# A channel-attention and ELU feed-forward kernel: joins of W' in two acts, the first pair's three v blocks cast on ScalarE, two output transfers in later units

## The chip, the cores and the metric

The kernel runs on 1 core of a Trainium2 chip. The core has five engines with a queue of instructions each: TensorE (PE; PEld is its weight load), VectorE (DVE), ScalarE (ACT), GpSimd (POOL) and SyncE (SP). SP and POOL issue nearly all the transfers here; one that casts or adds goes through POOL. An instruction waits at the head of its engine's queue, and everything behind it waits too. The metric is device time in microseconds (us). Before the change three runs took 2078.13, 2079.51 and 2080.13 us, median 2079.51.

## The reference

```python
qn = q / (np.linalg.norm(q, axis=1, keepdims=True) + 1e-06)      # q, k, v: (4, 6080, 256)
kn = k / (np.linalg.norm(k, axis=1, keepdims=True) + 1e-06)
s = kn.transpose(0, 2, 1) @ qn / tau                             # 256 x 256 for each batch
a = softmax(s)
x = (v @ a).reshape(24320, 256)
h = x @ w_in                                                     # w_in: (256, 2048)
g = np.where(h > 0, h, np.exp(np.minimum(h, 0)) - 1)
out = g @ w_out                                                  # w_out: (2048, 256)
```

The inputs q, k and v are float32. The kernel multiplies a and w_in first: W' = a w_in (256 x 2048 for each batch), so that h = v W'.

## The kernel before

Every float32 operand of a large product is split into a high part (rounded to the matrix format, fp32r) and a low part (the rest), and a product is three matmuls: high x high, high x low and low x high. High parts come from a ScalarE cast or from a casting transfer of GpSimd; low parts are a VectorE subtraction that reads the high part. Tokens go in 52 chunks of up to 512, 13 to a batch; W' has 16 blocks of 128 columns, in four quarters fq of 512.

Three stages matter here.

- **The opening** (to about 65 us) computes the attention matrix of batch 0 and the first quarter of W'.
- **64 steps** (`take`, 0 to 63) run the first four chunks the plain way. A step multiplies one block of W' with a chunk of v (`h_item`, L446 to L448: six matmuls into `ph`), applies ELU (ScalarE L457 and L458, VectorE L459), splits the block before it (`split_g`: ScalarE L114, VectorE L115) and multiplies the block three steps back with w_out (`out_item`, L486 to L490). What else has to be done, such as converting weights, squaring and adding batch 1's rows or preparing the next stage, is given to steps by `at(step, fn)`. Within a step the order of the code is the order of the queues.
- **Units**: the remaining 48 chunks go in 24 pairs of chunks (blocks of v B11, B12, B21, B22, and sums of them T1 to T4) against sums of W' blocks (S1 to S4, and A11, A12, A22), with seven products instead of eight. A pair has eight units (fq, j); a unit computes four blocks of h with `product` (L1161), applies ELU (L1238, L1239, L1242), splits the result (casting transfer L1256, low parts L1263 one unit later) and multiplies the unit before with w_out (L1171 to L1173). Between these, a planner puts side tasks into slots: `task(engine, cost, fn, deps, when, level, late, due)`; `when` is the earliest time (a unit has 4), lower levels go first, and a dependency may carry a gap. Each `spend(engine, budget, now)` in a unit issues what is ready.

The change touches what leads from the steps to the units:

- `join(fq)`: W' of batch 0 lies as high and low part in `wp`; the sums need it whole, so `x` (tiles x_0 to x_3 by fq) gets the high part by a copy of SyncE (L919, 512 KB) and the low part by an adding transfer of GpSimd (L920, 512 KB), which waits for the copy to land. Joins 0 and 1 stand in step 47, join 2 in step 59, join 3 is a planner's task. `s_sum` (VectorE, L844 to L847) then forms S1 to S4 in x, `s_hi` (GpSimd, L853, two casting transfers) and `s_lo` (VectorE, four subtractions L859) split the seven matrices into s_0 to s_3.
- The first pair: `first_pair_loaded` (step 45) loads v into two `exact` tiles, `hi_of` makes the high parts (of B22, B11 and B21 by a casting transfer out of HBM, L1086, in steps 47 to 49; of the T sums by ScalarE, L1088), `lo_of` (L1094) the low parts in steps 50 to 52, `t_sum` (L1074 to L1077) the T sums.
- `copy_out` for the last chunk of the steps adds two halves of 256 KB to the output with a transfer of GpSimd (L1191), issued where the copy out of PSUM is made, in unit 1.
- Also on GpSimd's queue: `add_row` (L875), which adds squares of batch 1 in this stage, and later the same by the planner (L1432).

The pools hand out room in rotation. s_0 takes the tile that held the first two quarters of W', s_2 that of the other two, s_3 that of `scr`, out of which the outputs of the first chunks go.

Of the kernel before, what the change touches and what calls it, by code (L numbers as in the profile page):

```python
# [7 lines left out]
F32 = mybir.dt.float32  # L8
# [3 lines left out]
ALU = mybir.AluOpType  # L12
# [42 lines left out]
def channel_attention_then_elu_ffn(ctx: ExitStack, tc, q, k, vT, tau, w_in, w_out, outT):  # L55
# [8 lines left out]
    nc = tc.nc  # L64
# [655 lines left out]
    def at(step, fn, free=False):  # L720
        (loose if free else side).setdefault(step, []).append(fn)
# [98 lines left out]
    def new_x(b, fq):  # L820
        if b > 0 and fq % 2 == 1:
            halves_of_x = [work.tile([P, 4, HF], F32, tag="raw", bufs=5, name=f"x_{b}_{fq}_{y}") for y in range(2)]
        else:
            x = work.tile([P, 8, HF], F32, tag="qk", bufs=3, name=f"x_{b}_{fq}")
            halves_of_x = [x[:, 0:4], x[:, 4:8]]
        state[b, "x", fq] = halves_of_x
# [58 lines left out]
    for x, g in enumerate((*range(KEPT, EARLY), *range(KEPT))):  # L885
        y = 10 + SPACING * x
# [25 lines left out]
    at(39, load_first_w)  # L912
    at(42, split_first_w)

    def join(fq):
        new_x(0, fq)
        wp = wps[0][fq]
        to = state[0, "x", fq][0].rearrange("p (k h) n -> p k (h n)", k=KT)
        nc.sync.dma_start(to, wp[:, :, 0].bitcast(F32))  # L919
        nc.gpsimd.dma_start(to, wp[:, :, 1].bitcast(F32), accum_op=ALU.add)  # L920

    at(47, lambda: join(0))
    at(47, lambda: join(1))
    for y in range(4):
        at(51 + y // 2, lambda y=y: s_sum(0, 0, y))
        at(56 + y // 2, lambda y=y: s_sum(0, 1, y))
    at(53, lambda: (new_s(0), room.append(spares[0]), [s_hi(0, 0, *p, True) for p in ((0, 3), (3, SPARE))]))
    for y, p in enumerate(PARTS):
        at(59 + y, lambda p=p: s_lo(0, 0, *p))
    at(59, lambda: join(2))  # L930

    steps = [(c, f) for c, lo, hi in pieces for f in range(lo, hi)]
    es, gs, pos = {}, {}, {}
# [51 lines left out]
    def task(engine, cost, fn, deps=(), when=0, level=1, late=None, due=None):  # L985

        t = Task(fn, tuple(d for d in deps if d is not None), when)
        t.late, t.engine = late, engine
        t.cost, t.due = cost, due
        if due is not None:  # L990
            level = 0
        queues[engine, level].append(t)
        return t
# [78 lines left out]
    def t_sum(p, k):  # L1072
        (
            lambda: nc.vector.tensor_sub(of(p, "T3"), of(p, "B22"), of(p, "B12")),  # L1074
            lambda: nc.vector.tensor_sub(of(p, "T1"), of(p, "B12"), of(p, "B11")),
            lambda: nc.vector.tensor_add(of(p, "T2"), of(p, "T3"), of(p, "B11")),
            lambda: nc.vector.tensor_sub(of(p, "T4"), of(p, "B21"), of(p, "T2")),  # L1077
        )[k]()

    def hi_of(p, term):  # L1080
        t0, n = columns(p)
        operands[p, term] = [room.pop(0)]
        to = operands[p, term][0][:, 0:n]
        if term in BLOCKS:
            kt, x = BLOCKS[term]
            nc.gpsimd.dma_start(to, vT[kt * P : kt * P + P, t0 + x * n : t0 + x * n + n])  # L1086
        else:
            nc.scalar.copy(to, of(p, term))  # L1088

    def lo_of(p, term):  # L1090
        n = columns(p)[1]
        operands[p, term].append(room.pop(0))
        hi, lo = (x[:, 0:n] for x in operands[p, term])
        nc.vector.tensor_sub(lo, of(p, term), hi.bitcast(F32))  # L1094
# [14 lines left out]
        room.extend(cut_up(work.tile([P, 4 * CH], F32R, tag="vt", bufs=2, name="t_0"), 4))  # L1109

    at(45, first_pair_loaded)
    at(47, first_pair_room)
    at(50, first_pair_next)
    for y, term in enumerate(("B22", "B11", "B21")):
        at(47 + y, lambda term=term: hi_of(0, term))
        at(50 + y, lambda term=term: lo_of(0, term))
    for y in range(4):
        at((53, 53, 55, 55)[y], lambda y=y: t_sum(0, y))
    at(57, first_pair_more)
    for x, y, term in ((56, 57, "T3"), (57, 59, "T2"), (58, 60, "T1"), (60, None, "T4")):  # L1120
        at(x, lambda term=term: hi_of(0, term))
# [64 lines left out]
    def copy_out(c, dt):  # L1186
        _, t0, n = span(c)
        if c < M:
            o, to = half[c][:, dt, 0:n], outT[dt * P : dt * P + P, t0 : t0 + n]
            nc.scalar.copy(quarters(o), quarters_of_turns(out_bank(c, dt)[:, 0:n]))  # L1190
            nc.gpsimd.dma_start(to, o, accum_op=ALU.add)  # L1191
            return
        assert all(len(y) == 2 for y in operands.values())
        x = exacts[dt][:, (c - M) % 2 * CH : (c - M) % 2 * CH + CH]
        o, to = x[:, 0:n], outT[dt * P : dt * P + P, t0 : t0 + n]
        if c == NCH - 1 and dt == DT - 1:
            m = n // 2
            y, z = o.rearrange("p (r t) -> p r t", r=2), out_bank(c, dt)[:, 0:n].rearrange("p (q r s) -> p r s q", r=2, s=2)
            y = y.rearrange("p r (s q) -> p r s q", s=2)
            nc.vector.tensor_copy(y[:, 0], z[:, 0])  # L1200
            nc.scalar.copy(y[:, 1], z[:, 1])
            nc.sync.dma_start(to[:, 0:m], o[:, 0:m])
            nc.scalar.dma_start(to[:, m:n], o[:, m:n])
        else:
            nc.scalar.copy(quarters(o), quarters_of_turns(out_bank(c, dt)[:, 0:n]))
            nc.sync.dma_start(to, o)
# [99 lines left out]
    def plan_s(b, fq, t, norm_deps, early=False):  # L1306
# [21 lines left out]
        hi = {}  # L1328
        if early and fq > 1:
            if fq == 3:  # L1330
                x = task(SP, 0, lambda: join(3), [(prior["lo before"], 1)], when=t, level=0, late=0)
            for k in range(4):
                x = task(DVE, 0.415, lambda k=k: s_sum(b, fq, k), [x and (x, 5) if k == 0 else x], when=t, due=t + 4, late=1)

# [405 lines left out]
```

## Time and profile before

| | before |
|---|---|
| median of 3 runs | 2079.51 us |
| the profiled execution | 2079.67 us, span 2077.9 us |
| DVE, ACT, POOL busy | 77%, 69%, 30% of the span |
| mean granted TensorE clock | 0.998 |
| transfers of POOL (q0) | 154592 packets, 295.05 MB |
| s<-x, 16 transfers of 512 KB, issue to landing | 4.9 us (median) |
| x<-wp of POOL, 4 transfers of 512 KB | 5.9 us (median) |

The span goes from the first to the last instruction. Busy time counts an engine while it executes; the idle time before an instruction is put down to what released it last. A row of the timeline gives start, duration, engine, line, operation, the tile written and the tiles read, and in brackets the idle time before it and its releaser. `x<-wp` means that x is written and wp read.

The 25 us stretches around the end of the steps (step 63 ends at 252 us, units follow) show TensorE's busy time with its matmuls, then PEld, DVE, ACT and POOL, the granted clock, the DMA engines' busy share and GB/s:

```profile
200.00:225.00 25.00, 18.86 (x86) 15.91 (x85) 15.11 (x23) 14.44 (x26) 7.33 (x9) 0.93 0.97 253
225.00:250.00 25.00, 25.00 (x109) 21.60 (x109) 24.23 (x43) 17.88 (x32) 1.42 (x2) 0.93 0.35 109
250.00:275.00 25.00, 23.41 (x105) 19.23 (x105) 19.95 (x35) 17.59 (x31) 9.75 (x15) 1.00 0.82 246
275.00:300.00 25.00, 20.58 (x88) 17.38 (x87) 17.56 (x31) 12.21 (x20) 8.60 (x17) 0.93 0.75 218
300.00:325.00 25.00, 25.00 (x118) 21.89 (x117) 22.73 (x37) 16.60 (x28) 5.70 (x11) 1.00 0.48 151
```

From 300 us on nearly every such stretch has TensorE busy throughout.

### The profile page before, as it was taken

The page shows a single profiled execution, that of the slowest core. Times are in us where ns is not written, and L with a number is a line of the kernel's source. Part 1 is how long each engine was busy: PE and PEld are TensorE (multiplying, and loading weights), DVE is VectorE, ACT ScalarE, POOL GpSimd, SP SyncE. Part 2 cuts the span into 40 slices and gives each one's busy share as a digit, 9 for nine tenths or more (in the row PEclk, how much of TensorE's full clock was granted, in tenths as well). Part 3 has the DMA queues.
Part 4 walks back from the last instruction along what each step waited for, and adds up shares of the span by engine and source line. Part 5 has one row for each costly group of instructions (what it writes and reads, how often), then busy time and mean ns, then how long its engine had stood idle before and what let it go on. Part 6 is the DMA issues. An engine that isn't in the chain of part 4 may idle for free.

```text
span 2077.9 us, 30137 instructions
## 1 busy us (share of the span) xinstructions
PE 2060.1 (99%) x9961; PEld 1826.6 (88%) x9961; DVE 1592.1 (77%) x2520; ACT 1429.2 (69%) x2420; POOL 625.5 (30%) x1084
## 2 busy tenths in 40 slices
PE   9999889999999999999999999999999999999999
PEld 8888778898888888888998888888998888888998
DVE  7878777777878777777778777777778867767775
ACT  6878657677666676766766667676776666666675
POOL 0011133442222444443222344443322222222221
PEclk9999999999999999999999999999999999999999
DMA  9357685994676989987457598997645653553533
GB/s 368 125 153 206 179 233 178 265 249 133 187 221 183 273 222 285 254 235 210 143 185 231 164 286 240 253 278 203 195 158 191 196 160 109 168 161 107 171 119 118
DMA packets 213339, 415.47 MB, mean 200 GB/s; under 512 B 23232, under 2 KB 68928, under 8 KB 211136
## 3 DMA queue, kind: packets, MB, share of 16 engines
q0 software_dynamic: 154592, 295.05, 50.2%
q1 hardware_dynamic: 58448, 118.39, 17.5%
q8 instruction: 78, 1.28, 0.3%
q14 instruction: 77, 0.63, 0.1%
q10 hardware_dynamic: 144, 0.13, 0.0%
HBM read 145.29 MB, written 30.15 MB: 84 GB/s over the span
## 4 chain that ended last, share of the span: by engine, by line
PE 92%; DMA 4%; issue 3%; DVE 1%; ACT 1%; POOL 0%; POOLq 0%; SPq 0%; DVEq 0%
PE bank_b L1161 16%; PE po L1172 14%; PE po L1173 14%; PE po L1171 14%; PE bank_e L1161 11%; PE bank_a L1161 11%; PE gram L225 4%; PE gram L574 2%; DMA sum<-raw 2%; PE pe L574 1%; PE ph L446 1%; PE ph L448 1%; PE ph L447 1%; PE po L490 1%; PE pw L816 0%
## 5 line engine op out<-in xcount | busy, mean ns | idle before, releaser
L1173 PE MATMUL po<-g,wo 128*128 128x512 f32 (+1 forms) x1416 | 535.3, 378 | 0.0
L1172 PE MATMUL po<-t,wo 128*128 128x512 f32 (+1 forms) x968 | 366.0, 378 | 0.0
L1171 PE MATMUL po<-t,wo 128*128 128x512 f32 (+1 forms) x968 | 365.0, 377 | 0.0
L1634 DVE TENSOR_TENSOR bank_e<-bank_b,p 128x512 f32<-128x512 f32 (+1 forms) x176 | 122.0, 693 | 282.0 <-PE bank_b L1161 271.5
L1173 PEld LDWEIGHTS po<-g,wo 128*128 128x128 f32 x1416 | 267.9, 189 | 34.6
L1624 ACT COPY bank_b<-bank_a 128x512 f32<-128x512 f32 (+1 forms) x176 | 99.5, 565 | 272.0 <-PE bank_a L1161 265.4
L1239 ACT ACTIVATE other<-other 128x512 f32<-128x512 f32 (+1 forms) x396 | 248.0, 626 | 12.6
L1256 POOL DMA_DIRECT2D t<-other x242 | 130.2, 538 | 419.3 <-DVE other L1242 256.3
L1256 POOL DMA_DIRECT2D t<-held x242 | 130.6, 542 | 287.8 <-DVE held L1242 117.6
L1171 PEld LDWEIGHTS po<-t,wo 128*128 128x128 f32 x968 | 183.0, 189 | 23.6
L1172 PEld LDWEIGHTS po<-t,wo 128*128 128x128 f32 x968 | 183.1, 189 | 22.6
L1239 ACT ACTIVATE held<-held 128x512 f32<-128x512 f32 (+1 forms) x308 | 193.2, 627 | 9.8
L1161 PE MATMUL bank_b<-t,s 128*128 128x512 f32 (+1 forms) x576 | 194.5, 379 | 5.1 <-DVE p L1651 5.1
L225 PE MATMUL gram<-qk 128*128 128x256 f32 x708 | 193.0, 273 | 0.0
L1256 POOL DMA_DIRECT2D g<-other x154 | 82.9, 539 | 326.9 <-DVE other L1242 182.1
L1172 PE MATMUL po<-g,wo 128*128 128x512 f32 (+1 forms) x448 | 170.4, 380 | 0.0
L1171 PE MATMUL po<-g,wo 128*128 128x512 f32 (+1 forms) x448 | 169.7, 379 | 0.0
L1263 DVE TENSOR_TENSOR g<-held,t 128x512 fp32r<-128x512 f32 (+1 forms) x242 | 162.2, 678 | 5.9 <-DMA t<-held 5.6
L1263 DVE TENSOR_TENSOR g<-other,t 128x512 fp32r<-128x512 f32 (+1 forms) x242 | 162.6, 679 | 0.5 <-DMA t<-other 0.5
L1238 ACT ACTIVATE other<-bank_a 128x512 f32<-128x512 f32 (+1 forms) x132 | 78.1, 592 | 117.1 <-PE bank_a L1161 112.5
L1161 PE MATMUL bank_b<-g,s 128*128 128x512 f32 (+1 forms) x432 | 147.1, 377 | 0.5 <-ACT bank_b L1624 0.5
L225 PEld LDWEIGHTS gram<-qk 128*128 128x128 f32 x708 | 135.4, 191 | 4.5
(288 smaller groups left out, 4920.7 us busy)
## 6 DMA issues: line engine op xcount, KB each, us to landing
t<-held POOLq DMA_DIRECT2D x154, 256.0 KB, 3.0
t<-other POOLq DMA_DIRECT2D x154, 256.0 KB, 2.7
acc<-raw POOLq DMA_DIRECT2D x118, 256.0 KB, 5.3
g<-other POOLq DMA_DIRECT2D x98, 256.0 KB, 2.3
t<-held POOLq DMA_DIRECT2D x88, 248.0 KB, 2.2
t<-other POOLq DMA_DIRECT2D x88, 248.0 KB, 2.2
raw<-in_q_dram SPq DMA_DIRECT2D x76, 256.0 KB, 3.6
raw<-in_k_dram SPq DMA_DIRECT2D x76, 256.0 KB, 4.2
```

Of the source, the lines that this page charges most:

```text
L225: yield nc.tensor.matmul(gram[:, ct, :], hl[:, x, 1, r, cs], in_turns(hl[:, y, 0, r, :]), start=(first and ct == 0 and r == 0 and k == 0), ...
L574: nc.tensor.matmul(gram[ct], raw[:, 1, r, ct * P : ct * P + P], raw[:, 0, r, :], start=first[ct], stop=last[ct])
L1161: nc.tensor.matmul(bank[:, 0:n], w[:, x], y, start=(begin and k == 0), stop=(k == 2), skip_group_check=True)
L1171: yield nc.tensor.matmul(o, wo[:, f, 0, ds], hi, start=begin, stop=False)
L1172: yield nc.tensor.matmul(o, wo[:, f, 1, ds], hi, start=False, stop=False)
L1173: yield nc.tensor.matmul(o, wo[:, f, 0, ds], lo, start=False, stop=end)
L1238: nc.scalar.activation(e, h, AF.Relu, scale=-1.0)
L1239: nc.scalar.activation(e, e, AF.Exp, scale=-1.0)
L1256: nc.gpsimd.dma_start(hi, e)
L1263: nc.vector.tensor_sub(lo, e, hi.bitcast(F32))
L1624: nc.scalar.copy(vb, va)
L1634: nc.vector.tensor_add(ve, vb, vp)
```

## The change

Three edits. (1) A join becomes two acts: the copy, and two steps later the adding transfer; copies now in steps 45, 47 and 59, additions in 47, 49 and 61; join 3's addition is a planner's task of GpSimd at level 0 that follows the copy by a gap of 2. (2) ScalarE casts the high parts of B22, B11 and B21 in steps 50 to 52 instead of three casting transfers in steps 47 to 49; their low parts come one step later (51 to 53), the t sums in steps 54, 55, 55 and 56, and the room for them is taken in step 50. (3) The two output transfers become tasks with earliest times 10 and 14, in units 2 and 3.

```diff
-    def join(fq):
-        new_x(0, fq)
+    def join(fq, x):
+        if x == 0:
+            new_x(0, fq)
         wp = wps[0][fq]
         to = state[0, "x", fq][0].rearrange("p (k h) n -> p k (h n)", k=KT)
-        nc.sync.dma_start(to, wp[:, :, 0].bitcast(F32))
-        nc.gpsimd.dma_start(to, wp[:, :, 1].bitcast(F32), accum_op=ALU.add)
-
-    at(47, lambda: join(0))
-    at(47, lambda: join(1))
+        if x == 0:
+            nc.sync.dma_start(to, wp[:, :, 0].bitcast(F32))
+        else:
+            nc.gpsimd.dma_start(to, wp[:, :, 1].bitcast(F32), accum_op=ALU.add)
+
+    for fq, y in enumerate((45, 47, 59)):
+        at(y, lambda fq=fq: join(fq, 0))
+        at(y + 2, lambda fq=fq: join(fq, 1))
...
-    at(59, lambda: join(2))
...
-    def hi_of(p, term):
+    def hi_of(p, term, by_act=False):
...
-        if term in BLOCKS:
+        if term in BLOCKS and not by_act:
...
-    at(47, first_pair_room)
+    at(50, first_pair_room)
     at(50, first_pair_next)
     for y, term in enumerate(("B22", "B11", "B21")):
-        at(47 + y, lambda term=term: hi_of(0, term))
-        at(50 + y, lambda term=term: lo_of(0, term))
+        at(50 + y, lambda term=term: hi_of(0, term, True))
+        at(51 + y, lambda term=term: lo_of(0, term))
     for y in range(4):
-        at((53, 53, 55, 55)[y], lambda y=y: t_sum(0, y))
+        at((54, 55, 55, 56)[y], lambda y=y: t_sum(0, y))
...
-            nc.gpsimd.dma_start(to, o, accum_op=ALU.add)
+            task(POOL, 0.6, lambda: nc.gpsimd.dma_start(to, o, accum_op=ALU.add), when=(10, 14)[dt], level=0)
...
-                x = task(SP, 0, lambda: join(3), [(prior["lo before"], 1)], when=t, level=0, late=0)
+                x = task(SP, 0, lambda: join(3, 0), [(prior["lo before"], 1)], when=t, level=0, late=0)
+                x = task(POOL, 0.6, lambda: join(3, 1), [(x, 2)], when=t, level=0)
```

Code behind the edits has moved by three or four lines (L1256 is L1259 after, L1094 is L1097). How the queues stand, at three places:

GpSimd's queue from step 47 on; x_0 and x_1 are the joins' tiles, acc<-raw the adding of squares, t<-in_v_dram the casts of the first pair, s the first split matrices. Before:

```order
L920 DMA x_0_1700<-wp_380 128x2x512
L920 DMA x_1_1703<-wp_380 128x2x512
L875 DMA acc_1728<-raw_712 128x512
L1086 DMA t_1706<-in_v_dram 128x512 x2
L875 DMA acc_1728<-raw_712 128x512
L1086 DMA t_1706<-in_v_dram 128x512
L853 DMA s_1848<-x_0_1700 128x768
```

and now:

```order
L923 DMA x_0_1639<-wp_380 128x2x512
L923 DMA x_1_1703<-wp_380 128x2x512
L875 DMA acc_1725<-raw_712 128x512 x2
L853 DMA s_1847<-x_0_1639 128x768
L875 DMA acc_1725<-raw_711 128x512 x2
```

The three casts have left this queue; the two adding transfers still stand one behind the other ahead of the rest. On SyncE's queue the copy of x_0 has moved past one load, that of k:

```order
L159 DMA raw_711<-in_q_dram 128x512
L921 DMA x_0_1639<-wp_380 128x2x512
L159 DMA raw_711<-in_k_dram 128x512
L921 DMA x_1_1703<-wp_380 128x2x512
L880 DMA acc_1725<-sum 128x1024
```

VectorE's queue in steps 50 and 51 (L459 ELU, L115 the low part of g, L1094 or L1097 a low part of the first pair, L844 and L845 the first sums of x_0). Before:

```order
L459 SCALAR_TENSOR_TENSOR e<-e,ph 128x512
L115 TENSOR_TENSOR g<-e,g 128x512
L1094 TENSOR_TENSOR t_1706<-exact_1640,t_1706 128x512
L459 SCALAR_TENSOR_TENSOR e<-e,ph 128x512
L115 TENSOR_TENSOR g<-e,g 128x512
L844 TENSOR_TENSOR x_0_1700<-x_0_1700 128x256
```

and now:

```order
L459 SCALAR_TENSOR_TENSOR e<-e,ph 128x512
L115 TENSOR_TENSOR g<-e,g 128x512
L459 SCALAR_TENSOR_TENSOR e<-e,ph 128x512
L115 TENSOR_TENSOR g<-e,g 128x512
L844 TENSOR_TENSOR x_0_1639<-x_0_1639 128x256
L845 TENSOR_TENSOR x_0_1639<-x_0_1639 128x256
L1097 TENSOR_TENSOR t_1773<-exact_1642,t_1773 128x512
```

The first low part has moved behind the first sums of x_0, which are now the first thing on this queue that reads a transfer's result.

GpSimd's queue from the end of unit 0 on (held and other are the blocks of h after ELU, t and g<-held or other their casts, out_dram<-scr the two outputs). Before:

```order
L920 DMA x_3_2190<-wp_381 128x2x512
L1191 DMA out_dram<-scr 128x512
L1256 DMA g_2167<-other_2092 128x512
L1191 DMA out_dram<-scr 128x512
L1256 DMA g_2167<-held 128x512
L1256 DMA t_2095<-held 128x512
L1256 DMA t_2095<-other_2090 128x512
L1086 DMA g_2167<-in_v_dram 128x512
L853 DMA s_2261<-x_2_1994 128x768
L853 DMA s_2261<-x_2_1994 128x1024
```

and now:

```order
L1259 DMA g_2167<-other_2092 128x512
L1259 DMA g_2167<-held 128x512
L1259 DMA t_2095<-held 128x512
L1259 DMA t_2095<-other_2090 128x512
L923 DMA x_3_2190<-wp_381 128x2x512
L1089 DMA g_2167<-in_v_dram 128x512
L853 DMA s_2259<-x_2_1993 128x768
L853 DMA s_2259<-x_2_1993 128x1024
L1259 DMA t_2095<-other_2091 128x512
```

Unit 1's four casts now stand ahead of join 3's adding transfer; the outputs have left for behind unit 2's and unit 3's casts, the second of them directly ahead of the loads and the s<-x of x_3.

## The prediction

> **What bounds the kernel now.** I read the busy shares first, then who TensorE waited for, then each of its two long gaps in order of time, and last the chain of waits through them. The first row is the page's busy time; the others give the wait in total, times and longest.
>
> ```profile
> PE 2060.1 (99%) x9961; PEld 1826.6 (88%) x9961; DVE 1592.1 (77%) x2520; ACT 1429.2 (69%) x2420; POOL 625.5 (30%) x1084
> PE po L490 <- DVE g L115: 6.0, 1, 6.0
> PE bank_b L1161 <- DVE p L1651: 5.1, 2, 4.4
> ```
>
> TensorE is busy for 2060.1 of 2077.9 us, so only its idle time, and time at a slower pace, can be won without taking out matmuls, and the change takes out none. Of the idle time 6.0 and 4.4 us are two single gaps. Everything here is about these two.
>
> **Gap 1**, TensorE's timeline (start, duration, line):
>
> ```profile
> 215.41 0.38 PE L486 MATMUL po<-g,wo 128*128 128x512 f32 x1
> ...
> 218.00 0.38 PE L486 MATMUL po<-g,wo 128*128 128x512 f32 x1
> 218.22 0.38 PE L488 MATMUL po<-g,wo 128*128 128x512 f32 x1
> 224.62 0.80 PE L490 MATMUL po<-g,wo 128*128 128x512 f32 x1 [6.03 <-DVE g L115]
> ...
> 228.68 0.38 PE L486 MATMUL po<-g,wo 128*128 128x512 f32 x1
> ```
>
> From 215.41 to 218.00 twelve matmuls start, one step in 2.59 us, 0.2158 us each. The matmul at 228.68 is the 11th after that of 218.22 and would have started at 218.22 + 11 x 0.2158 = 220.59. Gap 1 therefore costs **8.09 us**: 6.03 of idle time and 2.06 at half pace behind it. The 3 us after 225 (busy time of PE, PEld, DVE, ACT and POOL with instructions, granted clock, DMA share, GB/s) hold 8 matmuls at a clock of 0.50:
>
> ```profile
> 225.00:228.00 3.00, 3.00 (x8) 2.37 (x8) 3.00 (x7) 1.51 (x3) 0.87 (x1) 0.50 1.11 300
> ```
>
> What VectorE and the chain show there:
>
> ```profile
> 212.35 0.68 DVE L115 TENSOR_TENSOR g<-e,g 128x512 fp32r<-128x512 f32 x1
> 222.68 0.69 DVE L1094 TENSOR_TENSOR t<-exact,t 128x512 fp32r<-128x512 f32 x1 [9.64 <-DMA t<-in_v_dram]
> ```
> ```profile
> 205.49 5.60 DMA x<-wp
> ...
> 211.72 0.67 POOL x L920
> ...
> 214.66 7.99 DMA t<-in_v_dram
> ```
>
> VectorE stands 9.64 us at the low part of the first v block, because its high part is a casting transfer that GpSimd could issue only at 214.66: its queue stood at the adding transfer of join 0 until the copy of 205.49 had landed at 211.09.
>
> **Gap 2**, TensorE's timeline, the chain, and GpSimd's timeline behind it:
>
> ```profile
> 277.96 0.38 PE L1173 MATMUL po<-g,wo 128*128 128x512 f32 x1
> 282.76 1.54 PE L1161 MATMUL bank_b<-t,s 128*128 128x512 f32 x3 [4.42 <-DVE p L1651]
> ...
> 286.49 0.38 PE L1171 MATMUL po<-t,wo 128*128 128x512 f32 x1
> ```
> ```profile
> 264.54 4.62 DMA x<-wp
> ...
> 269.74 0.53 POOL x L920
> ...
> 272.15 8.03 DMA g<-held
> ```
> ```profile
> 276.26 0.53 POOL L853 DMA_DIRECT2D s<-x  x1 [0.75 <-DMA x<-wp]
> ```
>
> The row of 282.76 holds three matmuls, so that of 286.49 is the 10th after 277.96 and was due at 280.12: **6.37 us**. Here GpSimd stood at the adding transfer of join 3 until 269.74, then put it and two output transfers in among unit 1's casts; the cast g<-held issued at 272.15 needed 8.03 us, and VectorE's chain to L1651 waited for it. The profiled execution took 2079.67 us, 1.77 more than its span; the median, 2079.51, is 0.16 lower.
>
> **The change, part by part.**
>
> *Casts of the first pair on ScalarE.* Three casting transfers leave GpSimd's queue; three ScalarE casts come in, one in each of steps 50 to 52. A cast of that shape, and ScalarE's idle time in such a step:
>
> ```profile
> 215.61 0.60 ACT L457 ACTIVATE e<-ph 128x512 f32<-128x512 f32 x1 [0.69 <-PE ph L448]
> ...
> 235.73 0.62 ACT L1088 CAST t_o<-exact 128x512 fp32r<-128x512 f32 x1
> ```
>
> 0.62 us goes into an idle time of 0.69, so I cost it at nothing; without that cover it would be 3 x 0.62 = 1.9 us, spread over a lag of three steps. The 9.64 us wait goes, since nothing of these casts comes by GpSimd any more. Late next on VectorE is L844, the first sum of x_0, which needs join 0's adding transfer landed. From here on, times are on the old trace's clock.
>
> ```profile
> 203.82 0.33 SPq L159 DMA_DIRECT2D raw<-in_q_dram  x1
> ```
> ```profile
> x<-wp POOLq DMA_DIRECT2D x1, 512.0 KB, 5.6
> ```
> ```profile
> x<-wp POOLq DMA_DIRECT2D x1, 512.0 KB, 7.4
> ```
> ```profile
> 224.49 0.42 DVE L844 TENSOR_TENSOR x<-x 128x256 f32<-128x256 f32 x1
> ...
> 226.48 0.68 DVE L115 TENSOR_TENSOR g<-e,g 128x512 fp32r<-128x512 f32 x1
> ```
>
> *Join 0 in two acts.* The copy is moved one place up in SyncE's queue, past the k load, right behind the q load of 203.82: from 205.49 to 204.15. The adding transfer still waits for it and still heads GpSimd's queue, so the act of step 47 brings just these 1.3 us. It took 5.6 us from 211.72 (landed 217.3), join 1's 7.4. With 5.6 the sum lands near 216.0; with 7.4 and nothing gained, at 219.1. TensorE needs the low part made in step 52 at 218.44 + 2.59 = 221.03, and from L844 to the end of that L115 VectorE took 226.48 + 0.68 - 224.49 = 2.67: it must start L844 by 218.36. So the cost is 0 to 0.8 us; I take **0**, by the 5.6 of the same transfer. Joins 1 and 2, and the t sums one step later, move within this slack: their readers are four steps and more away.
>
> *Join 3 and the outputs behind the casts.* Unit 1's four casts now go out before join 3's adding transfer, and both output transfers leave for units 2 and 3. So the wait for g<-held goes. But gap 2 also hid something. The two transfers s<-x (L853) stand on GpSimd behind that adding transfer and wait for its landing, as the row of 276.26 shows, and VectorE's four L859 at the end of unit 2 read them. The rows for this: unit 1's last L1242, the same chain one unit on, the landing times of such transfers where they ran nearly alone, and the starts of units 3 and 4 (bank_a).
>
> ```profile
> 271.78 0.69 DVE L1242 SCALAR_TENSOR_TENSOR other<-other,p 128x512 f32<-128x512 f32 x1 [0.49 <-ACT other L1239]
> ...
> 286.23 2.22 DVE L859 TENSOR_TENSOR s<-x,s 128x256 fp32r<-128x256 f32 x4
> ...
> 288.82 0.42 DVE L845 TENSOR_TENSOR x<-x 128x256 f32<-128x256 f32 x1
> 290.65 0.70 DVE L1634 TENSOR_TENSOR bank_e<-bank_b,p 128x512 f32<-128x512 f32 x1 [1.40 <-PE bank_b L1161]
> ...
> 296.48 0.69 DVE L1242 SCALAR_TENSOR_TENSOR other<-other,bank_b 128x512 f32<-128x512 f32 x1 [0.17 <-ACT other L1239]
> ```
> ```profile
> x<-wp POOLq DMA_DIRECT2D x1, 512.0 KB, 4.9
> ```
> ```profile
> s<-x POOLq DMA_DIRECT2D x1, 512.0 KB, 3.2
> ```
> ```profile
> s<-x POOLq DMA_DIRECT2D x1, 512.0 KB, 4.6
> ```
> ```profile
> 287.79 0.38 PE L1161 MATMUL bank_a<-t,s 128*128 128x512 f32 x1
> ```
> ```profile
> 297.66 0.65 PE bank_a L1161 x3
> ```
>
> Without gap 2 unit 3 starts at 287.79 - 6.37 = 281.42, and L1634 is due 2.86 later (290.65 - 287.79), at 284.28. Unit 1's last cast follows 272.47 by about 0.5 (211.09 to 211.72 was 0.6), join 3's sum goes out at 273.5 and lands 4.9 later, 278.4; the two s<-x go at 278.9 and 279.5, and the second lands 3.2 to 4.6 later, 282.7 to 284.1. From there VectorE has the last two L859, L844 and L845 to do: the four L859 end at 288.45, the last two are 2 x 0.6 of it, and L845 ends at 289.24, so 289.24 - 287.2 = 2.05. It is ready at 284.75 to 286.2: 0.5 to 1.9 us late. I take the middle, **1.2**. Bounds: nothing if the sum lands in 3.2; with the 7.4 of the crowded transfer the second s<-x lands at 286.6, VectorE is 4.4 late, and at 4.4 us of idle time half pace follows (1.95 in gap 2): 6.3. Unit 2's own casts queue behind these two, and land at about 285, when VectorE reaches their low parts: no further cost.
>
> The Trainium skill, page "DMA: Bandwidth & Descriptors", section "Anatomy of one DMA — SWDGE (gpsimd) path", gives a GpSimd transfer 2.0 us plus its bytes at 436 GB/s, 3.2 us for 512 KB by estimate. By that rule the sum and s<-x would both take 3.2, VectorE would wait for nothing, and the time would be 1.2 us lower; the rows bear it out for one s<-x (3.2) and against it for every x<-wp (4.9 to 7.4).
>
> *The second output transfer.* s_3 takes scr's room, so s<-x of x_3 now waits on GpSimd until that output has landed, with unit 4's casts queued behind. Accumulating transfers of 256 KB:
>
> ```profile
> acc<-raw POOLq DMA_DIRECT2D x118, 256.0 KB, 5.3
> ```
> ```profile
> out_dram<-scr POOLq DMA_DIRECT2D x1, 256.0 KB, 8.0
> ```
>
> Unit 3 (from 282.6 with the 1.2) ends its last L1242 9.38 later (297.17 - 287.79), the output goes at 293.0 and lands D later; s<-x (0.5, 0.53, 4.6) and two L859 (1.2) are done at 299.8 + D, and L1634 of unit 5 is due at 282.6 + 2 x 9.87 + 2.86 = 305.2. The cost is D - 5.4: nothing at 5.3, 2.6 at the 8.0 of the crowded one. I take **0** by the 118 transfers of the first row.
>
> **Sum:** 2079.67 - 8.09 - 6.37 + 0 + 1.2 + 0 = **2066.4 us**, beside the median 13.1 us or 0.63% less. A measurement of this kernel tells about 0.2% (4.2 us) from no change.
>
> **Rivals.**
>
> 1. *Nothing follows gap 2*: join 3's sum lands in about 3 us, 2065.2. For it: transfers of SyncE are few after 273. Against it: no x<-wp under 4.9. Chance 0.20; the page's rule above leads here too.
> 2. *Gap 2 half comes back* as VectorE's wait for s<-x, because the sum takes 7.4 as in the crowd: 2065.2 + 6.3 = 2071.5. For it: the casts of unit 1 and the v block share its queue. Chance 0.16. The Trainium skill, page "TensorE: Matmul & The Clock Gate", section "Part 1: The HAM clock gate (the "warmup" mystery)", has half pace only after an idle window of about 3.4 us; by it a wait of 2 or 3 us would cost no more than itself, and the trace so far has just a gap of 4.42 that was followed by it.
> 3. *Gap 1 changes its releaser*: x_0's sum lands as late as the v casts did, and L844 starts at 222.68. Cost 222.68 + 2.67 - 221.03 = 4.3, and 2.0 of half pace: 2072.7. Chance 0.06; four transfers of 512 KB still share that stretch.
> 4. *The split does not do what it says*: the adding transfer in its act of two steps later finds its copy not landed and heads the queue as before, and L844 and the chain of unit 1 take over both gaps, so that only the copy's 1.3 us is won: 2078.4. Against it: the casts are out of that queue, and unit 1's stand ahead of join 3. Chance 0.04.
> 5. *Slower*: at both new heads of GpSimd's queue (s<-x behind join 3's sum, s<-x behind the second output) all casts of the next unit stand behind a landing. It turns the sign above 0.2% when both waits bring 14.46 + 4.2 = 18.7 us, 9.3 each with 2 of half pace: D - 5.4 + 2 is 9.3 at a landing of 12.7 us, and join 3's sum would need 11 us (1.2 + 11 - 4.9 + 2), against 4.9 to 8.0 seen. Then 2084 or more. Chance 0.02.
>
> **How the numbers follow.** The forecast, 2065.6 to 2068, has the remaining 0.52. The range goes from 2064.3 (rival 1, less the 0.7 that the second wait on L1651 has, 5.1 - 4.4, and the 0.16 to the median) to 2071.8 and takes in the forecast and rivals 1 and 2, about 0.88. Faster by over 0.2%: forecast and rivals 1 to 3, 0.94; within it, rival 4, 0.04; slower, 0.02.
>
> **What would show it.** Right: no TensorE gap over 2 us between 200 and 300; VectorE's L1094 of the first pair without a wait, L844 of x_0 with at most 2 us for x<-wp; L1263 of unit 2 without a wait; L859 at the end of unit 2 with 1 to 4 us for s<-x, followed by about 1 us on TensorE at bank_e or bank_b. Wrong: a gap of over 3.4 us with half pace behind it, at L490 (rival 3) or at unit 3 (rival 2), or a new wait in units 4 and 5 behind s<-x of x_3.

## The result and the profile after

The changed kernel takes **2066.8 us** (median of 4 runs, 2066.19 to 2068.09) against 2079.82 for the kernel before in the same session (4 runs, 2078.13 to 2081.98): a ratio of 0.9938, 95% interval 0.9920 to 0.9955. The forecast was 2066.4. The profiled execution took 2068.09, with a span of 2066.3, 11.6 less than the 2077.9 of before.

The page's busy times after, and the two longest entries of the list of who TensorE waited for (total, times, longest):

```profile
PE 2056.6 (100%) x9961; PEld 1824.8 (88%) x9961; DVE 1592.2 (77%) x2520; ACT 1430.3 (69%) x2423; POOL 624.2 (30%) x1081
PE bank_e L1164 <- DVE bank_e L1638: 2.0, 2, 1.8
PE bank_b L1164 <- DVE p L1655: 1.3, 3, 0.6
```

The matmuls are as many as before. The 6.0 at L490 is gone from the list, the 4.4 at bank_b is gone, and a wait of 1.8 at bank_e is new. By 25 us stretches (columns as in the table of before):

```profile
200.00:225.00 25.00, 24.89 (x116) 21.48 (x115) 22.66 (x37) 20.50 (x37) 6.99 (x8) 1.00 1.01 261
225.00:250.00 25.00, 24.41 (x113) 21.08 (x112) 23.10 (x41) 19.23 (x35) 1.07 (x2) 1.00 0.39 137
250.00:275.00 25.00, 24.01 (x108) 19.76 (x107) 19.41 (x33) 16.88 (x29) 9.42 (x15) 1.00 0.89 248
275.00:300.00 25.00, 23.20 (x108) 20.00 (x107) 21.92 (x38) 14.22 (x24) 10.40 (x19) 1.00 0.89 248
```

TensorE starts 116 matmuls from 200 to 225, where it started 86, and the granted clock is 1.00 in each of these stretches, where three of the four had 0.93. The DMA engines are no less busy: 1.01 where they were 0.97.

Three groups of rows show the rest: GpSimd's timeline at gap 1; VectorE's timeline from unit 2 on; and TensorE's at the new wait.

```profile
208.40 1.21 POOL L923 DMA_DIRECT2D x<-wp  x1 [10.93 <-DMA raw<-in_k_dram]
211.75 1.20 POOL L923 DMA_DIRECT2D x<-wp  x1 [2.15 <-DMA x<-wp]
212.97 1.78 POOL L875 DMA_DIRECT2D acc<-raw  x2
219.20 0.56 POOL L853 DMA_DIRECT2D s<-x  x1 [4.46 <-DMA x<-wp]
```
```profile
267.98 0.69 DVE L1266 TENSOR_TENSOR g<-held,g 128x512 fp32r<-128x512 f32 x1 [0.54 <-DMA g<-held]
...
275.59 1.03 DVE L859 TENSOR_TENSOR s<-x,s 128x256 fp32r<-128x256 f32 x2 [1.85 <-DMA s<-x]
276.97 1.29 DVE L859 TENSOR_TENSOR s<-x,s 128x512 fp32r<-128x512 f32 x2 [0.35 <-DMA s<-x]
...
278.98 0.69 DVE L1638 TENSOR_TENSOR bank_e<-bank_b,p 128x512 f32<-128x512 f32 x1
```
```profile
273.87 0.59 PE L1164 MATMUL bank_a<-t,s 128*128 128x512 f32 x2
...
279.72 0.48 PE L1164 MATMUL bank_e<-t,s 128*128 128x512 f32 x1 [1.80 <-DVE bank_e L1638]
...
285.65 0.59 PE L1164 MATMUL bank_a<-t,s 128*128 128x512 f32 x2
```

GpSimd still stands at the joins at gap 1 (2.15 us for join 1's copy, 4.46 at s<-x), but nothing that VectorE needs soon is behind them. In unit 2 VectorE waits 1.85 and 0.35 us for s<-x, and TensorE loses 1.80 at bank_e in unit 3.

The first matmul of unit 3 comes at 273.87 instead of 287.79, 13.92 earlier; that of unit 4 at 285.65 instead of 297.50, 11.85 earlier. So the new wait, with what stands around it, took 2.07 back, and the rest of the program kept 11.6.

### The profile page after: what moved, and what is told of

Its sections match the earlier page's. It is cut to its first block, busy times and chain, and to the rows that moved or that the text cites. A ratio compares the mean times of both kernels' runs of the same rounds, so it can differ in the third digit from the quotient of the medians.

```text
span 2066.3 us, 30138 instructions
## 1 busy us (share of the span) xinstructions
PE 2056.6 (100%) x9961; PEld 1824.8 (88%) x9961; DVE 1592.2 (77%) x2520; ACT 1430.3 (69%) x2423; POOL 624.2 (30%) x1081
## 4 chain that ended last, share of the span: by engine, by line
PE 96%; DVE 1%; DMA 1%; ACT 1%; issue 1%; POOL 0%; DVEq 0%; POOLq 0%
PE bank_b L1164 16%; PE po L1176 14%; PE po L1175 14%; PE po L1174 14%; PE bank_e L1164 11%; PE bank_a L1164 11%; PE gram L225 4%; PE gram L574 2%; PE ph L446 1%; PE ph L448 1%; PE ph L447 1%; PE po L490 1%; PE po L486 1%; PE pe L574 1%; PE po L488 1%; DMA t<-held 1%
## 5 line engine op out<-in xcount | busy, mean ns | idle before, releaser
L1638 DVE TENSOR_TENSOR bank_e<-bank_b,p 128x512 f32<-128x512 f32 (+1 forms) x176 | 122.1, 694 | 277.4 <-PE bank_b L1164 266.3
L1259 POOL DMA_DIRECT2D t<-other x242 | 129.0, 533 | 410.4 <-DVE other L1245 242.0
L1259 POOL DMA_DIRECT2D t<-held x242 | 129.5, 537 | 287.6 <-DVE held L1245 114.6
L1164 PE MATMUL bank_b<-t,s 128*128 128x512 f32 (+1 forms) x576 | 188.9, 378 | 0.8 <-DVE p L1655 0.8
L1259 POOL DMA_DIRECT2D g<-other x154 | 82.1, 533 | 332.1 <-DVE other L1245 185.1
L1266 DVE TENSOR_TENSOR g<-held,t 128x512 fp32r<-128x512 f32 (+1 forms) x242 | 162.3, 678 | 9.8 <-DMA t<-held 9.7
L1266 DVE TENSOR_TENSOR g<-other,t 128x512 fp32r<-128x512 f32 (+1 forms) x242 | 162.7, 679 | 0.0
```

The lines of the kernel that those rows point to most:

```text
L1164: nc.tensor.matmul(bank[:, 0:n], w[:, x], y, start=(begin and k == 0), stop=(k == 2), skip_group_check=True)
L1259: nc.gpsimd.dma_start(hi, e)
L1266: nc.vector.tensor_sub(lo, e, hi.bitcast(F32))
L1638: nc.vector.tensor_add(ve, vb, vp)
```

## The experiments

Two theories were put against each other. By the **queue theory** a gap is the time for which a transfer that waits for a landing stands at the head of GpSimd's queue with casts behind it. By the **load theory** it is the time that transfers take because they share the DMA engines; then bytes count, and not the order. Waits of TensorE over 0.3 us, from the timelines; the 0.6 that each profile has in units 0 and 1 is left out. "Held" is the cast g<-held of unit 1, issue to landing; "sum" is join 3's adding transfer, both from the list of transfers. Each ratio is to the kernel before in the same session, and the diffs below are against the changed kernel.

| kernel | median us (runs) | ratio to before, 95% | L490 | unit 2 | unit 3 | held | sum |
|---|---|---|---|---|---|---|---|
| before | 2079.51 (3) | 1 | 6.03 | 4.42 | | 8.0 | 6.2 |
| casts alone | 2073.11 (4) | 0.9965 (0.9952 to 0.9979) | | 5.72 | | 9.3 | 6.6 |
| joins alone | 2077.12 (10) | 0.9984 (0.9974 to 0.9993) | 4.83 | 3.61 | | 9.1 | 9.6 |
| outputs alone | 2074.01 (5) | 0.9968 (0.9956 to 0.9980) | 4.96 | 1.32 | | 6.0 | 6.0 |
| after | 2066.8 (4) | 0.9938 (0.9920 to 0.9955) | | | 1.80 | 6.6 | 6.9 |
| after, again | 2068.19 (5) | 0.9937 (0.9925 to 0.9950) | | | 2.35 | 6.6 | 7.4 |
| after, casts on GpSimd, early | 2066.89 (4) | 0.9936 (0.9923 to 0.9950) | | | 1.68 | 6.2 | 6.5 |
| after, outputs back | 2070.02 (5) | 0.9952 (0.9939 to 0.9964) | | 3.67 | | 9.1 | 9.7 |
| after, join 3 whole | 2066.36 (5) | 0.9932 (0.9919 to 0.9944) | | 1.39 | | 6.0 | 6.1 |
| after, sum early | 2066.86 (5) | 0.9933 (0.9921 to 0.9946) | | | 0.47 | 6.6 | 8.6 |
| after, loads late | 2072.96 (6) | 0.9967 (0.9955 to 0.9979) | | | 5.27 | 2.6 | 6.7 |
| after, sum early and loads late | 2064.45 (5) | 0.9923 (0.9909 to 0.9936) | | | | 2.7 | 4.9 |
| after, v block late | 2066.99 (5) | 0.9940 (0.9926 to 0.9954) | | | 1.64 | 6.3 | 6.5 |

### The three edits, each alone

Casts alone: the kernel before with ScalarE's casts; the joins in one act in their old steps, the outputs in unit 1.

```diff
+    at(47, lambda: (join(0, 0), join(0, 1)))
+    at(47, lambda: (join(1, 0), join(1, 1)))
...
-            task(POOL, 0.6, lambda: nc.gpsimd.dma_start(to, o, accum_op=ALU.add), when=(10, 14)[dt], level=0)
+            nc.gpsimd.dma_start(to, o, accum_op=ALU.add)
```

> The kernel before with the ScalarE casts alone (with their room, low parts and t sums in the later steps); joins in one act and outputs as before. Queue theory (the gaps come from what stands at the head of GpSimd's queue): gap 1 goes whole, 8.1 us, gap 2 stays at 6 to 6.4: about 2071.7 against 2079.8. Load theory (the gaps come from full DMA engines, so what counts is the bytes taken away, 0.77 MB at some 250 GB/s, 3.1 us): gap 1 shrinks to about 5 us with VectorE waiting at L844 for x_0's sum: about 2076.7.

Measured: 2073.11. TensorE's timeline has no wait at L490 any more, so these casts, with their low parts one step later, are enough to remove gap 1. Gap 2 stayed and grew to 5.72, behind a cast that VectorE awaited for 6.25 us:

```profile
275.89 1.65 PE L1164 MATMUL bank_b<-t,s 128*128 128x512 f32 x3 [5.72 <-DVE p L1654]
```
```profile
273.35 0.69 DVE L1266 TENSOR_TENSOR g<-held,g 128x512 fp32r<-128x512 f32 x1 [6.25 <-DMA g<-held]
```

Joins alone: the casts go back to GpSimd in steps 47 to 49 and the outputs to unit 1.

```diff
-        at(50 + y, lambda term=term: hi_of(0, term, True))
+        at(47 + y, lambda term=term: hi_of(0, term))
```

> The kernel before with the joins in two acts alone; the first pair's casts stay transfers, the outputs stay in unit 1. Queue theory: the three casts still stand behind both adding transfers, so gap 1 stays, less the 1 to 2 us by which the adding transfers start earlier (6 to 7 us); unit 1's casts pass join 3, so gap 2's wait goes or falls under 1 us and the wait of about 2 us for s<-x in unit 3 comes in: about 2074.4. Load theory: gap 1 and gap 2 as before, since the same bytes move in the same stretch: 2078 to 2080.

Measured: 2077.12, between the two; the ten runs spread from 2074.30 to 2079.89, so this median says less than the others. At gap 1 the split changes little, as the prediction had it: the two adding transfers still stand ahead of the casts. In unit 2 a wait of 3.61 is left although join 3's sum now goes out behind the casts, which the queue theory had not expected: the two outputs still stand between the casts, as GpSimd's timeline shows (the first row), and the cast behind them landed 9.1 us after its issue at 268.68.

```profile
268.11 1.23 POOL L1194 DMA_DIRECT2D out_dram<-scr  x1
268.68 1.21 POOL L1259 DMA_DIRECT2D g<-held  x1
```
```profile
280.33 1.03 PE L1164 MATMUL bank_b<-t,s 128*128 128x512 f32 x3 [3.61 <-DVE p L1655]
```

Outputs alone: joins and casts as before, the two output transfers in units 2 and 3.

```diff
-            nc.gpsimd.dma_start(to, o, accum_op=ALU.add)
+            task(POOL, 0.6, lambda: nc.gpsimd.dma_start(to, o, accum_op=ALU.add), when=(10, 14)[dt], level=0)
```

> The kernel before with the two output transfers in units 2 and 3 alone. Queue theory: gap 1 stays (8.1); in gap 2 GpSimd still stands at join 3's adding transfer until its copy has landed, then issues the casts without the outputs between, so 1 to 2 us of gap 2 stay, and no wait for s<-x in unit 3: about 2075. Load theory: gap 2 goes whole with the 0.5 MB: 2073.4.

Measured: 2074.01. The wait in unit 2 falls from 4.42 to 1.32 with join 3's sum still ahead of unit 1's casts. So **the outputs made most of gap 2**, and join 3's place about 1.3 of it. L490 waited 4.96 in this kernel and 6.03 in the one before although GpSimd's order is the same up to there: about 1 us at least is what this gap varies by between executions, and no experiment is read closer than that there.

```profile
278.91 0.92 PE L1164 MATMUL bank_b<-t,s 128*128 128x512 f32 x3 [1.32 <-DVE p L1654]
```

The gains alone, 7.2, 3.1 and 6.3 us against the kernel before in that session (2080.26), add up to 16.5; together they gave 13.0. A likely reason, not tested by itself, is that the second gap can be won only once and that the new wait in unit 3 belongs to none of the edits alone.

### Gap 1: the engine or the order

The changed kernel with the three casts back on GpSimd, the same bytes in the same stretch, but issued in step 46, behind one adding transfer instead of two.

```diff
-        at(50 + y, lambda term=term: hi_of(0, term, True))
+        at(46, lambda term=term: hi_of(0, term))
```

> The changed kernel with the first pair's three casts back on GpSimd, but given out in step 46, so that they stand behind one adding transfer (join 0) and ahead of join 1 and the squares; their low parts and the t sums as in the change. The same bytes move as before the change. Queue theory: casts issued at about 210 land by 217, VectorE waits under 2 us, no gap 1: about 2067, as the change. Load theory: the 0.77 MB are what costs, and a gap 1 of 4 to 5 us stays: 2071 to 2073.

Measured: 2066.89, and no gap 1. GpSimd's timeline and the first low part on VectorE:

```profile
208.16 1.21 POOL L923 DMA_DIRECT2D x<-wp  x1 [10.82 <-DVE g L115]
208.87 2.19 POOL L1089 DMA_DIRECT2D t<-in_v_dram  x3
```
```profile
218.20 0.69 DVE L1097 TENSOR_TENSOR t<-exact,t 128x512 fp32r<-128x512 f32 x1 [0.97 <-DMA t<-in_v_dram]
```

The casts go out at 208.87 instead of 214.66 and VectorE waits 0.97 instead of 9.64. That ScalarE does the casts isn't needed to remove the gap. But order alone is not all that differs from the joins alone, where the same casts stand behind both adding transfers: the low parts also come one step later here. The first cast took 9.3 us from 208.87 and landed at 218.2; with the joins alone it landed at 221.4, 3.2 later, and TensorE waited 4.83. In the kernel before TensorE went on 1.94 us after this low part began (222.68 to 224.62), and it was due at 218.44; a low part that begins at 218.20 in its old step would leave a wait of 1.5 to 1.7 us, by estimate from these rows. So the place in the queue makes most of the gap, and the later step the rest.

### Gap 2: outputs or join 3

Join 3 again in one act, ahead of unit 1's casts, in the changed kernel:

```diff
-                x = task(SP, 0, lambda: join(3, 0), [(prior["lo before"], 1)], when=t, level=0, late=0)
-                x = task(POOL, 0.6, lambda: join(3, 1), [(x, 2)], when=t, level=0)
+                x = task(SP, 0, lambda: (join(3, 0), join(3, 1)), [(prior["lo before"], 1)], when=t, level=0, late=0)
```

> The changed kernel with join 3 in one act again, its adding transfer ahead of unit 1's casts; joins 0 to 2, the casts and the outputs as in the change. Load theory, as the outputs-only kernel had it: a wait of about 1.3 us for g<-held in unit 2, and none in unit 3 because the sum lands 3 us earlier: 2066 to 2067, no different from the changed kernel, so join 3's own split is worth nothing. Queue theory: GpSimd's stand at the head costs as much as in gap 2 before, 4 to 6 us less the 2 of unit 3: 2069 to 2071.

Measured: 2066.36, the same as the changed kernel run beside it within the intervals. It has a wait of 1.39 in unit 2 and none in unit 3: the split of join 3 moves a loss of 1.4 to 2.4 us by one unit, and no gain of it can be measured.

```profile
271.28 0.92 PE L1164 MATMUL bank_b<-t,s 128*128 128x512 f32 x3 [1.39 <-DVE p L1654]
```

The changed kernel with the outputs back in unit 1 (the second line of the diff of the casts alone):

> The changed kernel with the two output transfers back in unit 1, between its four casts; the casts of the first pair on ScalarE and the joins in two acts stay. Theory 1, the outputs made most of gap 2, since they stand ahead of two of unit 1's casts and share the DMA engines with them: TensorE waits 2.5 to 4 us at the start of unit 2's products on bank_b (3.6 with the joins alone), VectorE's L1266 of unit 2 waits 2 to 6 us for g<-held, and the wait in unit 3 behind s<-x shrinks below 1 us, since join 3's sum is no later while the units are: 2068.5 to 2070.5 us. Rival, join 3's sum at the head of the queue made gap 2, and the outputs were only late riders: with the sum behind the casts no wait over 1 us in unit 2, 2066.5 to 2067.5.

Measured: 2070.02. The wait is back, and the cast g<-held took 9.1 us, as with the joins alone; the 3.6 of the expectation was 3.67. The cast took 8.0 to 9.3 us in the four kernels with the outputs in unit 1 and 2.6 to 6.6 in the others. Whether the outputs lengthen it by standing ahead of it or by the bytes that they move was not separated, so between the two theories gap 2 stays open.

```profile
273.15 1.65 PE L1164 MATMUL bank_b<-t,s 128*128 128x512 f32 x3 [3.67 <-DVE p L1655]
```

### The wait in unit 3: what made join 3's sum long

The sum took 6.9 us where the prediction had 4.9. First edit, **sum early**: the sum goes out by hand behind unit 1's second cast instead of its fourth.

```diff
-                x = task(POOL, 0.6, lambda: join(3, 1), [(x, 2)], when=t, level=0)
...
+        if u == 1:
+            join(3, 1)
```

> The changed kernel, with join 3's adding transfer issued in the middle of unit 1, behind its second cast, instead of behind its fourth. Queue theory: the copy has landed by then, GpSimd does not stand, the sum lands some 4 us earlier, VectorE's wait for s<-x at the end of unit 2 (2.2 us) and TensorE's 1.8 us in unit 3 go: about 2064.8 against the changed kernel's 2066.8. Load theory: the 512 KB then delay the two casts behind them, VectorE waits at L1266 in unit 2 by as much, and the time stays at 2066.8 or above.

Measured: 2066.86. The sum went out 4.1 us earlier (261.57) and landed only 2.5 earlier, since it took 8.6. The wait in unit 3 shrank to 0.47 in the profiled execution, the fastest of the five (2065.15), but the median didn't move beyond its interval, so the 2064.8 of the queue theory was missed. Then, together with it, **loads late**: SyncE's two loads of 512 KB for the second pair, under way at that time, go out on ScalarE's queue at the end of unit 2. A second profile of the changed kernel ran beside it. (The 8.3 us that the expectation gives for the sum is 8.6 in the list of transfers.)

```diff
+            if p == 0:
+                loads.append(task(ACT, 0.1, lambda kt=kt: load_pair(d, kt, nc.scalar), [state.get("t_lo")], when=t + 11, due=t + 11, late=1))
+                continue
```

> As join3_mid (join 3's adding transfer behind unit 1's second cast), and the second pair's two loads of 512 KB go out on ScalarE's queue at the end of unit 2, instead of on SyncE's queue in unit 1. Load theory: these loads share the DMA engines with the adding transfer, which took 8.3 us in join3_mid; without them it lands in about 5, s<-x at 267 to 268, VectorE waits neither at L1266 nor at L859: no TensorE wait over 0.7 us after the first, 0.5 to 1 us under join3_mid. Queue theory: the adding transfer keeps its 8 us, and the waits of join3_mid (0.5 to 1 us in units 2 and 3) stay.

> The changed kernel once more, beside the three below on the same chip. Queue and load theory alike: 2066.8 against some 2080, with TensorE's wait of about 1.8 us at bank_e in unit 3 and none over 1 us elsewhere after the first 2 us.

Measured: 2064.45 (2064.16 to 2065.35) against 2068.19 (2066.16 to 2068.79) for the changed kernel: it beats both kernels, with no wait over 0.6 us on TensorE after the first of 1.1. The sum took 4.9 us:

```profile
261.42 1.26 POOL L923 DMA_DIRECT2D x<-wp  x1
266.64 1.06 POOL L853 DMA_DIRECT2D s<-x  x2 [0.85 <-DMA x<-wp]
```

That looked like the load theory, with SyncE's loads as the cause. To see it alone, the loads were made late with the sum left in its place behind the fourth cast:

> The changed kernel with one edit: the two loads of 512 KB of the second pair's v go out on ScalarE's queue at the end of unit 2 instead of on SyncE's while join 3's sum is under way; join 3's sum stays behind unit 1's casts. Load theory: the sum took 6.9 us because those loads share its DMA engines, so it takes about 5 now, lands 2 us earlier, and the wait of 2.0 us in unit 3 falls below 0.5: 2064.5 to 2065.3. Rival, the sum's length is its own (the adding transfer reads and writes) and only its place counts: the wait in unit 3 stays 1.5 to 2.4, 2066.3 to 2067.5, and the best version needed the earlier place as well.

Measured: **2072.96**, about 6 us above the changed kernel, a clear miss. The sum still took 6.7 us, so taking SyncE's loads away did not shorten it. And the loads, issued 0.7 us ahead of the two s<-x, now lengthened those: the second took 7.0 us instead of 3.5. Timelines of the queues, VectorE and TensorE, and the list of transfers with their time to landing:

```profile
271.49 0.92 ACTq L1073 DMA_DIRECT2D exact<-in_v_dram  x2
272.22 1.05 POOL L853 DMA_DIRECT2D s<-x  x2 [5.09 <-DMA x<-wp]
...
278.43 1.03 DVE L859 TENSOR_TENSOR s<-x,s 128x256 fp32r<-128x256 f32 x2 [5.60 <-DMA s<-x]
...
282.48 0.79 PE L1164 MATMUL bank_e<-t,s 128*128 128x512 f32 x1 [5.27 <-DVE bank_e L1641]
```
```profile
x<-wp POOLq DMA_DIRECT2D x1, 512.0 KB, 6.7
```
```profile
s<-x POOLq DMA_DIRECT2D x1, 512.0 KB, 7.0
```

What the loads of SyncE do lengthen in the changed kernel is the cast g<-held: 6.6 us with them, 2.6 without. So sum early alone and loads late alone win nothing or lose, and together they win: early, the sum shares the DMA engines with the loads (8.6); late loads alone share them with s<-x.

Last, the v block: a casting transfer of 256 KB stands directly behind the sum. In the changed kernel it was moved behind unit 2's casts.

```diff
-        for term, when in zip(("B22", "B11", "B21"), (8, 9, 11)):
+        for term, when in zip(("B22", "B11", "B21"), (8 if p else 11, 9, 11)):
```

> The changed kernel with one instruction moved: the casting transfer of the second pair's first v block (256 KB out of HBM), issued 0.7 us behind join 3's sum, goes out behind unit 2's casts instead; SyncE's loads and the sum's place stay. Neighbour theory: the sum took 6.9 us because two casts stand directly ahead of it and this block directly behind it in GpSimd's own queue (SyncE's loads late leave it at 6.7); without the block it takes 4.9 to 5.8, the wait in unit 3 falls from 2.0 or 2.3 to 0 to 1.2, 2065 to 2066.3 us. Rival, the two casts ahead of it alone, or its place in the unit, make the length: 6.4 to 7, wait 1.7 to 2.4, 2066.5 to 2068.

Measured: 2066.99, sum 6.5, wait 1.64, close to the rival's numbers. With the block in place the sum took 6.9 and 7.4 in the two profiles of the changed kernel and 6.5 with the casts early, so this run shows no effect of the block that is clear of that spread. The cast directly ahead lands 4.6 us after its issue, at 269.7, and the sum 6.5 after its own, at 272.1, 2.4 later:

```profile
265.07 0.53 POOL L1259 DMA_DIRECT2D t<-other  x1 [0.66 <-DVE x L845]
265.59 1.26 POOL L923 DMA_DIRECT2D x<-wp  x1
```
```profile
t<-other POOLq DMA_DIRECT2D x1, 256.0 KB, 4.6
```

Yet a cast directly ahead is not enough to make the sum long. GpSimd's timelines with the loads late alone, and with the sum early and the loads late:

```profile
263.58 0.53 POOL L1259 DMA_DIRECT2D t<-held  x1 [2.10 <-PE po L1175]
264.76 0.53 POOL L1259 DMA_DIRECT2D t<-other  x1 [0.66 <-DVE x L845]
265.28 1.26 POOL L923 DMA_DIRECT2D x<-wp  x1
266.01 1.12 POOL L1089 DMA_DIRECT2D g<-in_v_dram  x1
```
```profile
260.90 0.53 POOL L1259 DMA_DIRECT2D g<-held  x1 [0.41 <-DMA x<-wp]
261.42 1.26 POOL L923 DMA_DIRECT2D x<-wp  x1
263.54 0.57 POOL L1259 DMA_DIRECT2D t<-held  x1 [0.86 <-PE po L1175]
```

In both the cast ahead goes out 0.52 us before the sum. In the first it took 4.2 us and the sum 6.7; in the second they took 2.7 and 4.9. The older cast of the first, t<-held, took 2.2 and had landed at 265.8, so it was not in the way for long. The nearest difference in the rows is what stands behind: the v block 0.7 us behind the sum, against a cast 2.1 us behind. So one run took SyncE's loads away and left the block, and the other took the block away and left the loads; that either one alone keeps the sum long is a rival that stands, and the changed kernel with both moved and the sum in its place was not run. What the rows do show is that the sum lands 2.4 to 3.0 us after the cast ahead of it in every kernel here that has one there. What makes that cast slow, and whether the sum waits for it or shares the engines with it, was not separated.

## Why the prediction was right, point by point

- **Gap 1, 8.09 us: right in size and cause.** The end of the steps comes 7.80 us earlier (the matmul at 252.21 stands at 244.41), in a run that was 0.30 later ahead of the gap (the same GpSimd transfer at 195.43 and 195.73), so 8.1. Casts alone showed that it is these casts, and the casts issued early that most of it is their place in the queue, the rest the step of their low parts.
- **ScalarE's casts, 0: right, but not by the cover that was named.** They took 0.60 to 0.61 us each. The idle time of 0.69 stands before the L457 of 215.61; the first cast came one step earlier, where ScalarE had none: the L457 of 213.18 in the kernel before follows the work ahead of it directly. The cast pushed this L457 back by 0.5 us (213.18 and the 0.30 are 213.48; it began at 213.99), and VectorE waited 1.94 for the L458 behind it, as the rows under this list show. TensorE lost nothing by it; it has no wait there. So what covered the cast must be the lag of three steps, which the prediction names beside the idle time.
- **Join 0's copy, 0 to 0.8, taken 0: right.** L844 waited for no transfer. The way there was partly luck: the sum went out at 208.40, 2 us ahead of the 210.4 implied (211.72 less 1.3), since the copy, issued at 203.74, took 4.1 where it took 5.6 before; but the sum then took 7.7 and not 5.6, so it landed at 216.1, close to the 216.0 of the forecast.
- **Gap 2, 6.37: right in size, loose in cause.** From the end of the steps to unit 3 the changed kernel gained 13.92 - 7.80 = 6.12. The prediction put join 3's stand first and named the outputs only as put in with it; the runs put the outputs first (4.42 to 1.32 without them) and join 3 second. Since the change moves both, the total came out all the same.
- **L1266 of unit 2 (L1263 before) without a wait: wrong, by 0.54 us**, because the cast g<-held took 6.6 us beside SyncE's loads; with the loads late it took 2.6 and this wait was gone. It cost at most the 0.25 that gap 2 fell short.
- **s<-x behind join 3's sum, 1.2: the mis-sized term.** It was 2.07. The mechanism was as told: VectorE waits for s<-x at L859 (1.85 + 0.35), TensorE follows at bank_e. The step that went wrong is the duration of the sum, taken as 4.9; it took 6.9 (7.4 in the second profile, where TensorE's wait was 2.35, above the 2 that the prediction allowed). The transfer of 4.9 did not run nearly alone, as the prediction has it: in the kernel before it goes out at 259.50 with casts 0.7 to 3.2 us behind it, but none ahead. This sum had two casts ahead of it on its own queue and the v block behind. The same transfer had taken 6.2 in the kernel before, a nearer row. The sum went out at 265.72, 7.8 earlier than the 273.5 on the old clock, just as predicted. The second s<-x took 3.5, within the 3.2 to 4.6, and landed at 276.97, 284.8 on the old clock, where 282.7 to 284.1 was forecast. L1638 began at 278.98, and was due 2.86 after unit 3's start, at 276.73: 2.25 late instead of 1.2.
- **The second output, 0: right.** s<-x of x_3 waited 2.63 us on GpSimd for the output, which took 4.1, and unit 5 starts 11.84 us earlier, as unit 4 does (11.85).

```profile
213.48 0.60 ACT L1091 CAST t<-exact 128x512 fp32r<-128x512 f32 x1
213.99 0.59 ACT L457 ACTIVATE e<-ph 128x512 f32<-128x512 f32 x1
```
```profile
215.27 0.69 DVE L459 SCALAR_TENSOR_TENSOR e<-e,ph 128x512 f32<-128x512 f32 x1 [1.94 <-ACT e L458]
```

In the profile the terms measured are 8.1 + 6.1 - 2.07 = 12.1 of the 13.26 predicted; the 0.3 at the start and about 0.2 over the remaining 1750 us lead to the 11.6. The terms as measured give about 2079.67 - 12.1, or 2067.5. That the median, 2066.8, lies within 0.4 of the forecast is partly luck: the four executions spread over 1.9 us, and the profiled one, 2068.09, was the slowest.

Of the rivals, the second has the mechanism that the runs came nearest to. With late loads alone it appeared at nearly the price worked out for it: 5.27 us of waiting and a clock of 0.50 behind it, 2072.96 against the 2071.5 of the rival. The transfer that was long there was s<-x (7.0 us instead of 3.5), not the sum. Where the sum did take the rival's 7.4, in the second profile of the changed kernel, s<-x took 3.5 and not the 4.6 of its price, and the wait was 2.35 without half pace. The prediction names a gap of 4.42 as the one that half pace had followed; in the same trace the gap of 6.03 was followed by it too, as its own rows at 225 show.

## What to carry to other kernels

In a queue that issues in order, price an edit by what stands ahead of the transfer that someone waits for, and give the transfers without a reader (outputs) a place behind those that have one. A transfer's duration holds for the neighbours that it had, here 4.9 us with none ahead and 6.9 with two; take it from a row with the same neighbours ahead and behind, on its own queue too. When two moves each win nothing alone, try them together before dropping both: here each had only pushed the collision to where the other was. The same goes for two neighbours that each seem harmless when taken away alone.

## What the hardware showed that was not expected

- **A transfer that adds or casts within the chip had no fixed time here.** The same 512 KB sum took 4.9 to 9.7 us in the kernels of the table, the same 256 KB cast 2.6 to 9.3. The Trainium skill, page "DMA: Bandwidth & Descriptors", section "Anatomy of one DMA — SWDGE (gpsimd) path", gives 3.2 us for 512 KB by estimate; s<-x with few neighbours agrees (3.5), no sum does.
- **Half pace had a length of its own here.** Waits of 1.80 and 2.35 left the clock at 1.00. With waits of 3.61 and more it fell to 0.50, and stayed there for about 3.4 us (waits of 3.61, 4.42 and 4.83) or about 6.8 (3.67, 4.96, 5.27, 5.72 and 6.03), as worked out from the mean clocks of one-us stretches. Two kernels with nearly equal waits, the joins alone (3.61) and the outputs back (3.67), show it; stretches with TensorE's busy time, clock, DMA share and GB/s, of the first and then of the second:

```profile
280.00:281.00 1.00, 0.67 (x3) 1.00 1.18 399
281.00:282.00 1.00, 1.00 (x4) 0.50 1.16 423
```
```profile
271.00:272.00 1.00, 0.00 (x0) 0.76 1.12 211
272.00:273.00 1.00, 0.00 (x0) 0.50 1.16 300
...
276.00:278.00 2.00, 2.00 (x6) 0.50 0.47 152
```

In the first the clock fell 4 us after the last matmul, as the work came back, and was back in full from 285; in the second it fell 2 us after the last matmul and stayed low to beyond 278. All eight cases go one of these two ways: where the clock fell 2.0 to 3.0 us after the last matmul it stayed low for 6.8, where it fell 4.3 to 4.6 after it for 3.4. The Trainium skill, page "TensorE: Matmul & The Clock Gate", section "Part 1: The HAM clock gate (the "warmup" mystery)", has the half pace come after an idle window of about 3.4 us that runs freely; the two lengths agree with such a window, but in the second kernel less than a whole one was idle when the clock fell. So the price of such a wait can't be read from its length alone: the same 3.6 us brought about 3.4 us at half pace with work in the one and about 5 in the other.
